# Attention and gated MLP on one core: the second product's matmuls taken block by block, exponentials planned into the buffer that is free first, and every step put in a new order

## The chip, the cores and the metric

The kernel runs on one core of a Trainium2 chip. A core has a matrix engine (TensorE, PE in the profile; its weight loads are PEld), VectorE (DVE), ScalarE (ACT), GpSimd (POOL) and SyncE (SP, which here issues all DMAs). Each engine works through its own instruction queue in order and waits on semaphores for the others. The metric is the device time of one execution in microseconds (us), the median of several runs.

## The reference, cut to what matters

```python
def _attn_ref(q, k, v, g_q, g_k):            # batch 8, heads 12, seq 448, head_dim 64
    q_n, k_n = rmsnorm(q, g_q), rmsnorm(k, g_k)
    scores = matmul(q_n, k_n.transpose(0, 1, 3, 2)) / sqrt(64)
    attn = exp(scores - max(scores))
    attn = attn / (sum(attn) + 1e-9)
    return matmul(attn, v)
...
def _moe_ref(x, w_in, conv_w, w_out):        # x 8 x 448 x 768, w_in 768 x 1024, w_out 1024 x 768
    h = maximum(x @ w_in, 0.0)
    conv_out = 3-tap convolution of h along the sequence, one set of taps per column
    gate = 1.0 / (1.0 + exp(-conv_out))
    return (h * gate) @ w_out
```

## The kernel before, in words

The work is cut into small steps, each a function: a call for one tile on one engine. A helper `at(t, fn, ...)` puts a step on a list with a due time made of a formula in `PH`, `PACE` and a shift per kind of step (`SHIFT`). A planner at the end of the kernel then builds one order for each engine: it keeps, for every engine, the steps whose predecessors (`needs`) are placed, adds up planned costs (`options`: a step's planned time on each engine that may take it; `LAT`: the planned delay from one engine to another; `OVER`: the part of a step's planned time by which the next step on the same engine may overlap it), and places the step that can start first, with due times weighted by `beta`. What it builds is an order and nothing else: on the chip each engine takes its instructions in that order and waits where an operand is late.

Heads go two at a time, a pair n (48 pairs, six to a batch). For a pair, q and k are loaded and normalised (`square`, `square_sum`, `rsqrt`, `apply_rms`), transposed by PE (`qk_transpose`) or, for q of later pairs, by a DMA (`q_turn`), and split into a high and a low float16 part (`qk_hi`, `qk_lo`). `scores(n, g)` multiplies them into PSUM for the row blocks of 128 queries, seven blocks j = 0..6 to a pair. Each block goes through `soft_max` (DVE, the row's negated maximum), `soft_exp` (ACT, into one of four buffers with tag `e`), and is then turned: in pairs 0 to 9 all blocks by PE (`p_transpose`, copied out of PSUM by `p_evac`), from pair 10 on the first six (even pairs) or five (odd pairs) by a split into two float16 halves (`p_hi`, `p_lo`) and a DMA (`p_turn`), and only the last block or two by PE. `pv(n, i)` multiplies with v, `x_scale` divides by the row sums (which come back through DRAM, tile rB), `x_hi` and `x_lo` split the result in two float16 parts, tile x.

The MLP of batch b: `in_part(b, fc, j, w)` is w matmuls of the first product for column block fc (0..7); its index i runs over the six pairs' x (i // 3) and for each over three terms: high times high, low times high, high times low (table `T3`). Six such steps fill one PSUM bank. Then `in_relu`, three steps `in_conv`, `in_tanh`, `in_gate`, which frees the bank, and `in_hi`, `in_lo`, which write the gated block in two parts g into a ring of slots (`gring` and two spare places). The second product, `out_part(b, ch, half, j, w)`, takes 24 matmuls in six steps of four for each output tile. Its order before, line 909, is term by term: all eight blocks of the high part, then the low parts, then the high parts with the low weights, so that its second step already needs block 7. All matmul outputs share eight PSUM banks, which are handed out by the planner: a step that takes a bank waits until the last reader of its former content is done.

Weights w_in and w_out are loaded, converted and bounded at the start (`load`, `convert`, `bound`, `bound_max`, `bound_turn`, `bound_spread`, `scale`, `split`, `rest`) between the attention steps of the first pairs.

Two lines that the change replaces and the prediction uses, with the planned costs of before:

```python
            soft_exp=lambda: [act(0.645)],
...
    OVER = dict(PE=0.0, DVE=0.08, ACT=0.1, POOL=0.035)
```

## Time and profile before

| | us |
|---|---|
| median of 3 runs | 844.54 |
| lowest and highest | 844.24 and 846.04 |
| span of the profiled execution | 844.4 |
| PE busy in it | 799.5 |
| DVE, ACT, POOL busy | 701.8, 698.1, 517.7 |

The profiled execution's span, from the first to the last instruction, is within 0.2 us of the median, so the trace's sums can be set against the median directly. A busy share is the part of the span in which at least one instruction of that engine was in flight; PE's matmuls overlap each other, so its busy time contains short waits that no gap shows. The start of one instruction to the start of the next (the pitch) is what a matmul really takes.

### The profile page before, as it was taken

The page shows a single profiled execution, that of the slowest core. Times are in us where ns is not written, and L with a number is a line of the kernel's source. Part 1 is how long each engine was busy: PE and PEld are TensorE (multiplying, and loading weights), DVE is VectorE, ACT ScalarE, POOL GpSimd, SP SyncE. Part 2 cuts the span into 40 slices and gives each one's busy share as a digit, 9 for nine tenths or more (in the row PEclk, how much of TensorE's full clock was granted, in tenths as well). Part 3 has the DMA queues.
Part 4 walks back from the last instruction along what each step waited for, and adds up shares of the span by engine and source line. Part 5 has one row for each costly group of instructions (what it writes and reads, how often), then busy time and mean ns, then how long its engine had stood idle before and what let it go on. Part 6 is the DMA issues. An engine that isn't in the chain of part 4 may idle for free.

```text
span 844.4 us, 17078 instructions
## 1 busy us (share of the span) xinstructions
PE 799.5 (95%) x5650; PEld 435.0 (52%) x5650; DVE 701.8 (83%) x1298; ACT 698.1 (83%) x1647; POOL 517.7 (61%) x633
## 2 busy tenths in 40 slices
PE   3897999999999999999999999999999999999998
PEld 2454455545554555555555555555545555555554
DVE  7889988997899889998889988998789989781430
ACT  4889999989899887999898987998898987893441
POOL 4445246487678667597577767697667767572120
PEclk9998999999999999999999999999999999999999
DMA  9684553169997899869997898979996899555001
GB/s 255 180 197 122 172 147 109 45 137 197 180 194 173 163 193 200 167 141 196 197 177 161 182 200 186 179 150 199 183 187 154 185 184 169 108 106 112 10 18 58
DMA packets 325640, 132.47 MB, mean 157 GB/s; under 512 B 265312, under 2 KB 321968, under 8 KB 325552
## 3 DMA queue, kind: packets, MB, share of 16 engines
q1 hardware_dynamic: 325552, 131.39, 75.0%
q8 instruction: 44, 0.72, 0.4%
q14 instruction: 44, 0.36, 0.1%
HBM read 56.65 MB, written 11.18 MB: 80 GB/s over the span
## 4 chain that ended last, share of the span: by engine, by line
PE 38%; ACT 24%; DVE 17%; DMA 9%; issue 7%; POOL 4%; SPq 2%; ACTq 0%; DVEq 0%; POOLq 0%
PE bank L917 15%; PE bank L848 8%; PE bank L764 6%; PE bank L642 5%; DMA rB<-rd 4%; ACT ph L98 3%; PE bank L686 3%; ACT sq L385 2%; DMA PT<-ph 2%; DMA wo<-in_moe_w_in_dram 2%; DVE vp L748 1%; ACT PT L98 1%; POOL ph L110 1%; ACT bank L856 1%; SPq L678 1%
## 5 line engine op out<-in xcount | busy, mean ns | idle before, releaser
L848 PE MATMUL bank<-x,wi 128*128 128x448 f16 x1152 | 233.8, 353 | 0.0
L917 PE MATMUL bank<-wo,gring 128*128 128x384 f16 (+1 forms) x1056 | 203.4, 327 | 1.8 <-DVE c_(0_7_1979 L878 1.7
L848 PEld LDWEIGHTS <-wi 128*128 128x128 f16 x1152 | 110.9, 98 | 99.3 <-issue 7.6
L917 PEld LDWEIGHTS <-gring 128*128 128x128 f16 (+1 forms) x1056 | 101.6, 99 | 67.6 <-issue 16.3
L642 PE MATMUL bank<-kT,qT 64*128 64x448 f16 (+3 forms) x1072 | 131.8, 395 | 4.1 <-ACT qT L98 3.4
L764 PE MATMUL bank<-PT,vp 112*64 112x448 f16 x912 | 93.7, 354 | 0.8 <-DVE c_(5_4_8472 L878 0.4
L110 POOL TENSOR_TENSOR x<-x,x 128x448 f16<-128x448 f32 x48 | 52.9, 1102 | 45.3 <-ACT x L98 33.3
L110 POOL TENSOR_TENSOR sq<-qkf,st 112x512 f32<-112x512 f32 x61 | 72.1, 1191 | 8.5 <-DVE st L417 5.1
L764 PEld LDWEIGHTS <-vp 112*64 112x64 f16 x912 | 50.2, 110 | 41.3 <-issue 12.6
L396 DVE TENSOR_REDUCE st<-sq 112x16 f32<-112x1024 f32 (+1 forms) x50 | 58.2, 1168 | 7.0 <-ACT sq L385 6.5
L642 PEld LDWEIGHTS <-qT 64*128 64x128 f16 (+1 forms) x912 | 32.7, 97 | 51.8 <-issue 32.1
L385 ACT ACTIVATE sq<-qkf 112x1024 f32<-112x1024 f32 (+1 forms) x50 | 51.1, 1022 | 4.2 <-DMA qkf<-in_q_dram 2.3
L917 PE MATMUL bank<-wo,wi 128*128 128x384 f16 (+1 forms) x192 | 46.9, 326 | 0.0
L456 PE MATMUL bank<-ident,sq 112*128 112x112 f32 x232 | 32.4, 267 | 14.4 <-POOL sq L110 13.9
L775 DVE TENSOR_TENSOR x<-bank,rB 128x448 f32<-128x448 f32 x38 | 23.6, 622 | 25.2 <-PE bank L764 9.9
L702 DVE TENSOR_TENSOR PT<-bank,PT 112x512 f16<-112x512 f32 x57 | 39.0, 684 | 4.3 <-ACT PT L98 3.9
L856 ACT ACTIVATE bank<-bank 128x448 f32<-128x448 f32 x64 | 34.1, 534 | 7.3 <-PE bank L848 6.6
L748 DVE SCALAR_TENSOR_TENSOR vp<-v,vsc,vp 112x512 f16<-112x512 f32 x38 | 39.8, 1047 | 0.2 <-ACT vp L102 0.2
L98 ACT COPY PT<-bank 112x512 f32<-112x512 f32 x64 | 36.9, 590 | 3.5 <-PE bank L686 3.4
L110 DVE TENSOR_TENSOR sq<-qkf,st 112x512 f32<-112x512 f32 x35 | 38.7, 1131 | 0.0
L709 POOL TENSOR_SCALAR rsum<-rsum 128x7 f32<-128x7 f32 x48 | 17.5, 365 | 33.5 <-ACT e_(3_6_774 L656 7.5
L98 ACT CAST x<-x 128x448 f16<-128x448 f32 x45 | 25.2, 560 | 15.5 <-DVE x L775 14.8
(2228 smaller groups left out, 2021.8 us busy)
## 6 DMA issues: line engine op xcount, KB each, us to landing
qkf<-in_k_dram SPq DMA_DIRECT2D x48, 224.0 KB
v<-in_v_dram SPq DMA_DIRECT2D x48, 224.0 KB
rB<-rd SPq DMA_DIRECT2D x96, 112.0 KB
wo<-in_moe_w_in_dram SPq DMA_DIRECT2D x12, 512.0 KB
gring<-in_moe_w_out_dram SPq DMA_DIRECT2D x16, 384.0 KB
qkf<-in_q_dram SPq DMA_DIRECT2D x24, 224.0 KB
qkf<-in_q_dram SPq DMA_DIRECT2D x48, 112.0 KB
PT<-ph SPq DMA_TRANSPOSE x209
```

Of the source, the lines that this page charges most:

```text
L98: (nc.scalar.copy if e == "ACT" else elementwise(e).tensor_copy)(dst, src)
L110: elementwise(e).tensor_tensor(dst, a, b, op=op)
L385: nc.scalar.activation(sq, x, AF.Square)
L396: nc.vector.tensor_reduce(st, sq, axis=AX.X, op=ALU.add)
L456: nc.tensor.transpose(ps[:, t * PB : (t + 1) * PB], x[:, t], ident[:PB, :PB])
L642: nc.tensor.matmul(ps[u][o, :S], lhs, rhs, start=(i == 0), stop=(whole(m) or i == 2),)
L702: nc.vector.tensor_tensor(turned(n, j, 1), held["t", ("p", n, j)][:PB].rearrange("p (k q) -> p k q", k=NB), turned(n, j, 0), op=ALU.subtract,)
L748: nc.vector.scalar_tensor_tensor(vp[:, 1], old("v", n), old("vsc", n // NP)[:PB, 1:2], vp[:, 0], op0=ALU.mult, op1=ALU.subtract,)
L764: nc.tensor.matmul(ps[HALF[h], :S], lhs, rhs, start=(i == 0 and k == 0), stop=(i == pvs(n)[-1] and k == NB - 1),)
L848: nc.tensor.matmul(ps[:, :S], wi[:, wl, c, fc * P : (fc + 1) * P], old("x", b * NP + c)[:, xl], start=(i == 0), stop=(i == 3 * NP - 1),)
L856: nc.scalar.activation(ps, ps, AF.Relu, scale=2.0 ** -24)
L917: nc.tensor.matmul(ps[p0 : p0 + m, :NO2], g, wo[:, wl, fc, half * NO2 : (half + 1) * NO2], start=(i == 0), stop=(i == 3 * NFC - 1),)
```

## The change

Three things change in the code and all numbers of the tables.

1. `out_part` walks a new list `OUT`: for each block fc its three terms (high with both weight parts, then low), where before it went term by term over all blocks. A step of four then needs the blocks up to (j + 3) // 3 only, and a slot of g is free for the next batch once the last two `out_part` steps that read its block are done; before, it was once the whole second product of the batch was done.
2. `needs` of `in_part` asks for the x of the pair that its matmuls read; before, it asked for the x of all six pairs. `x_hi` asks for the last `in_part` step that reads its own pair.
3. The planner's rule for the four exponential buffers changes: before, an exponential waited in the plan for the buffer of the exponential four places earlier; now it waits for the first one of those in use that is freed.
4. Planned costs (`options`, `LAT`), a factor for each engine (`COST`) and `PH`, `PACE`, `SHIFT` are all new, so all steps are placed anew.

```diff
-    sw=0.0, f_pl=0.052, f_ql=0.872, f_lo=0.172, f_rms=0.091, f_sq=0.309, T=17.368, ti=41.151,
+    sw=-0.0213, f_pl=0.0039, f_ql=-14.6094, f_lo=0.2593, f_rms=0.1033, f_sq=0.3016, T=17.5428,
...
+COST = dict(
+    PE=0.9855, DVE=1.0004, ACT=1.0007, POOL=1.0014,
+)
...
+    OUT = [(fc, gl, wl) for fc in range(NFC) for gl, wl in ((0, 0), (0, 1), (1, 0))]
...
-            gl, wl = T3[i // NFC]
-            fc = i % NFC
+            fc, gl, wl = OUT[i]
...
-            m, j = back(n, a[1], BUFS["e"])
-            yield ("p_lo" if j < nd(m) else "p_transpose"), m, j
...
-            yield "in_part", (n - BUFS["x"]) // NP, NFC - 1, 3 * NP - 3, 3
+            yield "in_part", (n - BUFS["x"]) // NP, NFC - 1, n % NP * 3, 3
...
-            for i in range(NP):
-                yield "x_lo", b * NP + i
+            for c in range(j // 3, (j + m - 1) // 3 + 1):
+                yield "x_lo", b * NP + c
...
-            pb = back(b, a[1], NGS, NFC)[0]
-            yield "out_part", pb, 3 if pb % 2 else 2, 1, 3 * NFC - 4, 4
-            yield "in_carry", *back(b, a[1], NGS, NFC)
+            pb, pf = back(b, a[1], NGS, NFC)
+            for half in range(2):
+                yield "out_part", pb, 3 if pb % 2 else 2, half, (3 * pf + 2) // 4 * 4, 4
+            yield "in_carry", pb, pf
...
-            soft_exp=lambda: [act(0.645)],
+            soft_exp=lambda: [act(0.725)],
...
-            p_low=lambda: [dve(0.63)],
+            p_low=lambda: [dve(0.683)],
...
-            in_part=lambda: [pe(0.58)],
+            in_part=lambda: [pe(0.568)],
...
-            out_part=lambda: [pe(0.67)],
+            out_part=lambda: [pe(0.65)],
...
-        "PE": dict(PE=0.0, DVE=0.2, ACT=0.2, POOL=0.2, SP=0.2, DMA=0.2),
+        "PE": dict(PE=0.0, DVE=0.2062, ACT=0.1869, POOL=0.8133, DMA=0.32, SP=0.32),
...
+                if step[0] == "soft_exp" and exps >= BUFS["e"]:
+                    if exps - BUFS["e"] >= len(freed):
+                        continue
+                    t = max(t, back_at(freed[exps - BUFS["e"]], e, dma))
...
+        c = c if dma else c * COST[e]
```

The same 4976 steps are placed, 1265 of them on PE with the same matmuls. Which engine takes an elementwise step changes for a few dozen: among others `out_evac` moves from DVE to ACT five times and `sum_evac` eleven times, twelve `in_carry` go from ACT to DVE, five `q_lo` from DVE to POOL, three `apply_rms` from POOL to DVE. PE changes between kinds of products (`scores`, `pv`, everything else) 271 times before and 289 times now.

What moves is seen at three places of PE's queue. Line numbers of after are 4 or 5 higher than those of before for the same statement. The first place is the transposition of the last block of pair 38, e_(38_6. L642 (L646) are `scores`, L848 (L853) `in_part`, L686 (L690) `p_transpose`. Before:

```order
L642 MATMUL bank_67<-kT_7973,qT_8029 64x448
...
L642 MATMUL bank_73<-kT_7973,qT_8029 128x448
...
L848 MATMUL bank_69<-x_7933,wi_84 128x448
...
L848 MATMUL bank_68<-x_7011,wi_84 128x448
...
L686 MATMUL bank_66<-ident,e_(38_6_8224 112x128 x4
...
L848 MATMUL bank_68<-x_7316,wi_84 128x448
```

And after, at the same place:

```order
L853 MATMUL bank_70<-x_7945,wi_84 128x448
...
L853 MATMUL bank_66<-x_7033,wi_84 128x448
...
L460 MATMUL bank_73<-ident,sq_7891 128x112 x4
...
L853 MATMUL bank_66<-x_7288,wi_84 128x448
...
L646 MATMUL bank_71<-kT_8003,qT_8058 128x448
...
L853 MATMUL bank_66<-x_7506,wi_84 128x448
...
L853 MATMUL bank_66<-x_7726,wi_84 128x448
...
L853 MATMUL bank_73<-x_6826,wi_84 128x448
...
L690 MATMUL bank_68<-ident,e_(38_6_8255 112x128 x4
```

Before, the block's own scores (the rows with 64 in them hold half of it), one more scores step and two `in_part` steps of three matmuls stand ahead of the transposition; now the block's scores lie ahead of everything shown, and twelve `in_part` steps (not all shown), a `qk_transpose` and a scores step stand between.

The second place is the start of batch 0's second product, L917 (L921), on the banks that it is written to. Before:

```order
L642 MATMUL bank_72<-kT_1864,qT_1737 128x448
...
L917 MATMUL bank_67<-wo_85,gring 128x384
...
L456 MATMUL bank_66<-ident,sq_1606 128x112 x4
L686 MATMUL bank_70<-ident,e_(10_6_2032 112x128 x4
...
L917 MATMUL bank_73<-wo_85,gring 128x384
...
L917 MATMUL bank_67<-wo_85,gring 128x384
```

After:

```order
L768 MATMUL bank_72<-PT_1611,v_735 64x448 x8
...
L921 MATMUL bank_69<-wo_85,gring 128x384
...
L690 MATMUL bank_68<-ident,e_(10_6_2021 112x128 x4
L460 MATMUL bank_71<-ident,sq_1768 128x112 x4
...
L646 MATMUL bank_72<-kT_1758,qT_1655 128x448
...
L921 MATMUL bank_69<-wo_85,gring 128x384
L921 LDWEIGHTS gring
L921 MATMUL bank_71<-wo_85,gring 128x384
```

Before, one step of the first output tile is followed by a step into bank_73, the bank that held the first product's block 7; now four steps of the first tile come first, the second tile goes to bank_71, and no block of the first product is the last user of either bank.

The third place is the first `in_part` of the kernel, about 95 to 125 us into the span, among the transpositions of pairs 5 to 7. Before:

```order
L686 MATMUL bank_70<-ident,e_(5_4_1047 112x128 x4
L642 MATMUL bank_73<-kT_973,qT_1002 128x448
...
L686 MATMUL bank_70<-ident,e_(5_5_1061 112x128 x4
L686 MATMUL bank_69<-ident,e_(5_6_1071 112x128 x4
L686 MATMUL bank_68<-ident,e_(6_0_1092 112x128 x4
...
L686 MATMUL bank_73<-ident,e_(7_4_1279 112x128 x4
L848 LDWEIGHTS wi_84
L848 MATMUL bank_71<-x_618,wi_84 128x448
```

After:

```order
L690 MATMUL bank_72<-ident,e_(5_4_1047 112x128 x4
...
L853 MATMUL bank_68<-x_533,wi_84 128x448
...
L853 MATMUL bank_68<-x_738,wi_84 128x448
L690 MATMUL bank_66<-ident,e_(5_5_1063 112x128 x4
L719 MATMUL bank_71<-ident,rsum_940 7x128
...
L853 MATMUL bank_68<-x_847,wi_84 128x448
...
L690 MATMUL bank_70<-ident,e_(5_6_1073 112x128 x4
```

Before, the first `in_part` follows block 4 of pair 7; now three steps of it stand between blocks 4 and 6 of pair 5, and three more between there and block 4 of pair 7.

## Rows read from the trace of the kernel before

**Rows 1.** The page's first part: engine, busy us (share), instructions.

```profile
PE 799.5 (95%) x5650; PEld 435.0 (52%) x5650; DVE 701.8 (83%) x1298; ACT 698.1 (83%) x1647; POOL 517.7 (61%) x633
```

**Rows 2.** Busy time by stage: stretch, length, then each engine; PEclk is the granted clock.

```profile
0.00:10.32 10.32, 0.00 (x0) 0.00 (x0) 6.08 (x24) 4.10 (x7) 3.87 (x14) 1.00 0.73 210
10.32:130.00 119.68, 104.12 (x595) 58.15 (x596) 110.75 (x238) 107.63 (x270) 53.15 (x80) 0.96 0.68 177
130.00:800.00 670.00, 654.44 (x4771) 353.04 (x4768) 576.87 (x1026) 572.88 (x1348) 455.46 (x535) 1.00 0.81 160
800.00:844.40 44.40, 40.90 (x289) 23.80 (x287) 8.10 (x13) 13.50 (x25) 5.18 (x5) 1.00 0.10 36
```

**Rows 3.** Timeline of PE, 742 to 757 us: start, us, instruction, count.

```profile
742.82 3.00 PE L848 MATMUL bank<-x,wi 128*128 128x448 f16 x15
745.66 0.27 PE L715 MATMUL bank<-ident,rsum 128*7 128x128 f32 x1
745.86 1.43 PE L642 MATMUL bank<-kT,qT 64*128 64x448 f16 x18
...
752.86 3.42 PE L917 MATMUL bank<-wo,gring 128*128 128x384 f16 x20
756.12 0.27 PE L715 MATMUL bank<-ident,rsum 128*7 128x128 f32 x1
756.23 2.76 PE L917 MATMUL bank<-wo,gring 128*128 128x384 f16 x16
```

**Rows 4.** PE's waits from 130 to 800 us: us in total, times, longest.

```profile
PE bank L917 <- DVE c_(0_7_1979 L878: 1.7, 1, 1.7
...
PE bank L686 <- ACT e_(13_5_2619 L656: 1.0, 1, 1.0
PE bank L686 <- ACT e_(38_6_8224 L656: 0.9, 1, 0.9
...
PE bank L917 <- ACT e_(16_5_3316 L656: 0.4, 1, 0.4
...
PE bank L686 <- ACT e_(29_5_6234 L656: 0.2, 1, 0.2
```

**Rows 5.** Timeline of ACT, 626 to 627 us: one exponential and what follows it.

```profile
626.20 0.66 ACT L656 ACTIVATE e_(39_3_8368<-bank,sst_(39_3_8352 128x448 f32<-128x448 f32 x1
...
626.82 0.58 ACT L98 CAST gring<-c_(5_1_8288 128x448 f16<-128x448 f32 x1
```

**Rows 6.** Timeline of PE, 180 to 187 us, where batch 0's second product starts.

```profile
180.58 0.65 PE L686 MATMUL bank<-ident,e_(10_6_2032 128*112 128x128 f32 x4 [0.18 <-ACT e_(10_6_2032 L656]
182.93 4.06 PE L917 MATMUL bank<-wo,gring 128*128 128x384 f16 x24 [1.70 <-DVE c_(0_7_1979 L878]
```

**Rows 7.** Timelines of DVE and PE, 65 to 78 us, and one stretch's busy row.

```profile
65.10 0.61 DVE L648 TENSOR_REDUCE sst_(3_5_725<-bank 128x1 f32<-128x448 f32 x1
...
68.13 0.27 PE L190 MATMUL bank<-ident,wred_in 128*1 128x128 f32 x1 [3.46 <-DVE wred_in L287]
...
72.22 1.10 PE L686 MATMUL bank<-ident,e_(3_3_671 128*112 128x128 f32 x4
...
77.74 0.65 PE L686 MATMUL bank<-ident,e_(4_0_818 128*112 128x128 f32 x4
78.23 0.60 PE L686 MATMUL bank<-ident,e_(4_1_824 128*112 128x128 f32 x4
...
72.22:75.82 3.60, 3.60 (x18) 3.26 (x17) 3.40 (x11) 2.80 (x6) 2.02 (x5) 0.50 1.09 227
```

**Rows 8.** Timeline of PE, 120 to 126 us; last, the w_in halves on line L312.

```profile
120.53 1.02 PE L642 MATMUL bank<-kT,qT 64*128 64x448 f32 x4 [1.07 <-ACT qT L98]
...
123.74 1.86 PE L848 MATMUL bank<-x,wi 128*128 128x448 f16 x9
...
L312 DVE SCALAR_TENSOR_TENSOR wi<-wi,wsc x6: 1270/1284/1511, 75.0 to 96.7; 128x1024 f16<-128x1024 f32 x6
```

**Rows 9.** All waits, one of DVE's rows.

```profile
DVE x L775 <- DMA rB<-rd: 9.4, 10, 2.6
```

More of the change, by code (lines that the diff above doesn't have):

```diff
@@ L28 @@
+    p_qh=1.3778, p_ql=5.1453, p_ph=15.3737, p_pl=18.0701,
 )
 PACE = [
-    19.684, 19.21, 17.229, 18.732, 12.899, 14.504, 12.3, 10.264, 22.811, 17.751, 23.834, 17.246,
+    19.6835, 17.2279, 17.1001, 19.4583, 13.0839, 14.5901, 12.3383, 10.1304, 23.241, 17.8279, 22.0846, 15.8073,
 ]
 SHIFT = dict(
-    prepare=49.118, load_g=66.183, make_g=161.271, load_cw=41.777, make_cw=228.436, load=30.589,
-    convert=88.08, bound=185.211, bound_max=505.945, bound_turn=109.494, bound_row=36.478,
-    bound_spread=103.145, scale=368.594, in_factor=602.484, split=143.452, rest=-5.433,
@@ L36 @@
-    out_factor=26.564, load_k=207.53, load_q=-22.481, square=411.214, square_sum=340.919,
-    rsqrt=50.152, apply_rms=498.265, qk_transpose=555.031, qk_hi=86.942, v_load=355.244,
-    v_bound=-7.228, scores=24.319, soft_max=-4.096, soft_exp=21.811, p_transpose=365.136,
-    p_evac=1.005, sum_add=366.28, sum_step=2.99, sum_transpose=104.607, sum_evac=262.686,
-    sum_store=184.116, sum_load=7.026, pv=384.832, x_scale=90.761, x_hi=276.516, x_lo=5.432,
-    v_max=-27.973, v_turn=484.625, v_row=103.578, v_spread=219.686, v_scale=143.146,
@@ L42 @@
-    qk_lo=-5.353, q_hi=-16.467, q_lo=93.092, q_turn=368.336, p_hi=513.085, p_lo=-4.651,
-    p_turn=292.059, p_low=-2.554, v_hi=204.989, v_lo=184.473, moe_scales=122.854,
-    in_part=120.167, in_relu=338.096, in_conv=209.998, in_tanh=27.902, in_gate=21.022,
-    in_hi=197.514, in_lo=1.938, in_carry=175.792, out_scales=185.546, out_part=267.736,
-    out_evac=257.905, out_store=1.003,
+    prepare=695.9036, load_g=605.045, make_g=537.5802, load_cw=507.761, make_cw=1158.5217,
+    load=31.6554, convert=120.3172, bound=646.657, bound_max=1897.893, bound_turn=288.6078,
@@ new lines @@
+    bound_row=964.8649, bound_spread=187.7733, scale=1072.724, in_factor=1018.0854,
+    split=742.8313, rest=-5.4893, out_factor=1386.2035, load_k=292.4823, load_q=-22.4572,
+    square=669.9932, square_sum=728.8853, rsqrt=1200.7674, apply_rms=1327.5481,
+    qk_transpose=1487.4879, qk_hi=51.7292, v_load=195.6348, v_bound=-6.2815, scores=102.7029,
+    soft_max=-4.2547, soft_exp=175.5778, p_transpose=64.7604, p_evac=0.5117, sum_add=63.9685,
+    sum_step=1281.1798, sum_transpose=442.8909, sum_evac=286.0047, sum_store=534.9805,
@@ new lines @@
+    sum_load=-0.73, pv=279.316, x_scale=196.1933, x_hi=1476.0933, x_lo=5.043, v_max=-27.0337,
+    v_turn=1369.8103, v_row=682.245, v_spread=716.8841, v_scale=1686.192, qk_lo=-11.3264,
+    q_hi=-16.4621, q_lo=1098.9752, q_turn=1358.9663, p_hi=431.7814, p_lo=-5.142, p_turn=7.7804,
+    p_low=-1.725, v_hi=856.9811, v_lo=140.521, moe_scales=314.8581, in_part=1449.2977,
+    in_relu=1462.579, in_conv=787.5631, in_tanh=144.9106, in_gate=772.8823, in_hi=507.0311,
+    in_lo=4.5699, in_carry=174.6416, out_scales=357.2239, out_part=29.3667, out_evac=289.1293,
@@ L47 @@
+    out_store=-6.4416,
+)
+COST = dict(
+    PE=0.9855, DVE=1.0004, ACT=1.0007, POOL=1.0014,
 )
@@ L1250, in needs @@
             yield "in_lo", *a
-            yield "out_part", b - 3, 0, 1, 3 * NFC - 4, 4
+            for half in range(2):
+                yield "out_part", b - 3, 0, half, 3 * NFC - 4, 4
         elif name == "out_part":
@@ L1309, in options @@
             v_scale=lambda: [dve(0.7)],
-            scores=lambda: [pe(0.77 if whole(a[0]) else 0.585)],
+            scores=lambda: [pe((0.912 if whole(a[0]) else 0.691) if a[0] % 2 and not a[1] else 0.847 if whole(a[0]) else 0.578)],
             soft_max=lambda: [dve(0.62)],
-            soft_exp=lambda: [act(0.645)],
-            p_transpose=lambda: [pe(0.455)],
-            p_low=lambda: [dve(0.63)],
-            p_evac=lambda: [act(0.59), dve(0.62)],
+            soft_exp=lambda: [act(0.725)],
+            p_transpose=lambda: [pe(0.436)],
+            p_low=lambda: [dve(0.683)],
+            p_evac=lambda: [act(0.585), dve(0.682)],
             sum_add=lambda: [pool(0.3), dve(0.09)],
@@ L1431, in tile_attention_moe, with frees_e @@
     ringq = {"m": [], "c": [], "t": [], "s": []}
+    exps, freed = 0, []
+    def frees_e(name, *a):
+        return name == "p_transpose" and a[1] >= nd(a[0]) or name == "p_lo"
     most = dict(s=PH["cs"], t=PH["ct"], m=PH["cm"], c=BUFS["c"])
@@ L1518, in tile_attention_moe @@
                     last_in[i] = g
+        exps += step[0] == "soft_exp"
+        if frees_e(*step):
+            freed.append(step)
         order.append(step)
```

63 lines of the change are left out of this document (31 added, 32 removed).

## The prediction

> **What bounds the kernel now.** I read the page's busy shares first. PE is in flight for 799.5 of 844.4 us; DVE, ACT and POOL lie 140 us and more below it [rows 1]; weight loads, 52%, run beside the matmuls. By stage [rows 2] that splits in four. Until 10.32 us PE has nothing. From 10.32 to 130 us PE idles 15.6 us (119.68 less 104.12) while DVE and ACT are busy for 93% and 90% of the stretch: there those two set the pace. From 130 to 800 us PE idles 15.6 us more, and DVE and ACT have 14% free. The last 44.4 us are PE alone, with 3.5 us of evacuation and store behind it. So a new order can give back some of about 31 us of visible idle time, plus what hides inside PE's busy time.
>
> For that the pitch is needed [rows 3]. Fifteen matmuls of the first product take 745.66 - 742.82 = 2.84 us, 189 ns each, 0.568 us a step of three. Twenty of the second take 756.12 - 752.86 = 3.26 us, 163 ns each, 0.652 us a step of four. One such matmul is in flight for 0.33 to 0.35 us, so each of PE's waits hides another 0.17 us or so in the busy time. The same rows price a change between kinds of products: the transposition of the row sums takes 0.11 us when a full product follows (756.12 to 756.23) and 0.20 us when scores follow (745.66 to 745.86), so 0.09 us for the change.
>
> **Where PE waits from 130 to 800 us.** The list of PE's waits [rows 4] has 26 entries that add up to 15 us. Sixteen of them, from 1.0 to 0.2 us and 9.6 us together, are `p_transpose` (L686) waiting for the exponential of block 5 or 6. The four matmuls of such a step are in flight for 0.65 us where the next step can start 0.49 us after them [rows 7], so each wait hides another 0.16 us: about 12 us in all. Three waits of L917 and two of L642, 0.2 to 0.4 us, are for the bank of a late exponential; two of L764 are of 0.4 us, not shown; and the largest, 1.7 us, is batch 0's second product waiting for `in_gate` of block 7.
>
> Why the exponentials are late can be worked out. Before, the plan gave one 0.645 us less the overlap of 0.1, so 0.545 us of ACT; the trace gives 626.82 - 626.20 = 0.62 us [rows 5]. Seven to a pair make 0.5 us that ACT falls behind its plan. PE was planned too slow: 0.67 against 0.652 and 0.58 against 0.568 us [rows 3], with eight steps of each to a pair (384 over 48 pairs) 0.14 + 0.10 = 0.24 us. PE comes 0.76 us early to a transposition for each pair's work, and the larger waits, 0.7 to 1.2 us with their hidden part, have that size. The new costs are 0.725 less 0.1, 0.65 and 0.568 us, the trace's own.
>
> **The change part by part.** The matmuls are the same, so the pitch costs nothing.
>
> *Changes of kind*: 289 instead of 271, 18 at 0.09 us: +1.7 us. Nothing hides this, PE being the bound.
>
> *Transpositions placed by true costs*: of about 12 us, between none (the waits only move to the next step) and all can go. In PE's queue, counted with the pitches above, the work between a block's scores and its transposition grows from 1.9 to 8.1 us for e_(38_6 and from 1.9 to 6.1 us for e_(13_5, of the rows shown; of the nine largest waits six get at least 0.7 us more, two stay within 0.2 us, one (18_6) drops from 5.0 to 2.1 us. I take six in ten: -7 us, the rest staying because DVE's and ACT's durations vary more than a plan can know.
>
> *Second product block by block*: the start of batch 0's [rows 6] costs 182.93 - 180.58 = 2.35 us where a transposition's four matmuls take 0.49, so 1.9 us. Now four steps of the first output tile (2.6 us) come first, no bank of it is one that the first product's last block held, and the step that needs block 7 has 12.9 us of PE's work between it and that block, where it had 7.6. The same holds for the waits of L917 in odd batches, of 0.2 to 0.4 us, with 0.17 us hidden in each. Bounds 0 and 3.2 us; -2.5 us, nearest to the one row with a whole mechanism. That a slot of g frees earlier is worth nothing: no row of PE's waits is for a slot.
>
> *Early part*: `bound_turn` waits 3.46 us for DVE's maximum [rows 7]. In DVE's new queue three instructions less stand ahead of it, two maxima of 0.61 us and a conversion: -1.5 us, bounds 0 and -3.46. [...]
>
> *First product earlier*: it starts at 123.74 us, although w_in's last part, 1.3 us long, began at 96.7 us [rows 8], because its rule wanted the x of all six pairs. Six steps of 0.568 us now stand ahead of that place, in a stretch where PE waits on ACT, at 120.53 us for 1.07 us. 3.4 us of work can lie in idle time that lasts anyway; I take -2 us. If w_in is not ready, those steps wait and hold the transpositions behind them: loss to 1 us.
>
> *Other waits* (L642, L764) go by the same cause: -1 us of 1.4.
>
> *New waits*: an `in_part` that takes the bank of a `pv` stands at least 1.3 us of PE's work behind it, and eight do so where four did, at 3.0 us or more; that bank is free once `x_scale` is done, and `x_scale` itself waits for rB, 9.4 us in ten times and 2.6 us at worst [rows 9]. The last pair's x has 14 us of PE's work before its use in the middle case, where it had 21. Between 0 and 2.6 us at each; I allow +2 us in all, since before, DVE's waits for rB delayed no PE step in the list.
>
> *Buffers of exponentials*: no instruction changes, and ACT has 14% free; 0 us. Moves of `out_evac`, `sum_evac` and others between DVE and ACT are under 12 of 1280 steps and change neither share: 0 us while both have that room, and some 5 us at 0.3 to 0.6 us each if they had not.
>
> *Sum*: 844.4 + 1.7 - 7 - 2.5 - 1.5 - 2 - 1 + 2 = 834.1 us. The profiled execution stands within 0.2 us of the median, so I predict **834 us**, its own range 828 to 840.
>
> **The rivals.**
>
> *Nearly all waits go.* The 12 us of transpositions, 3.2 of the second product, 3.46 and 1.6 us at `bound_turn`, 3.4 us of filled idle time and 1.4 us of others: 844.4 + 1.7 - 25.1 = 821.0 us. For it speaks that the error of the plan has just the size of the waits; against it that 18_6 moves closer and that DVE and ACT stay the pace until 130 us.
>
> *Slower: PE stops for x.* The queue is strict, so an `in_part` that waits for a bank of `pv` or for the last pair's x holds every transposition behind it, and ACT and DVE run dry after. Sixteen places (eight banks, eight batches) at 1.5 us each are 24 us in place of the 2 allowed: 844.4 + 1.7 - 14 + 24 = 856 us. It decides from 0.8 us a place on, where sixteen waits make up the 14 us of gains less the 1.7. The spacing of 1.3 us and the waits for rB speak for it; against it, that most of the sixteen have 5 us and more.
>
> *No change.* ACT and DVE, not the plan's error, make the exponentials late: then each wait comes back at the next transposition and only the second product's gain, the changes of kind and half of the new waits remain: 844.4 + 1.7 - 2.5 + 1 = 844.6, within 0.2% of before, which is about what a measurement of this kernel can tell from no change. Their 14% of free time speaks against it.
>
> **How the numbers follow.** The forecast (828 to 840) has 0.60; nearly all waits gone, or between it and the forecast, 0.15; a gain that stays smaller (840 to 842.8) 0.07; no change 0.05; slower 0.13. Faster by over 0.2% is then 0.60 + 0.15 + 0.07 = 0.82, same 0.05, slower 0.13. The range leaves out the lowest tenth, below 821, and the worst tenth, above 848.
>
> **What would show it.** In the changed profile PE's idle time from 130 to 800 us is 5 to 9 us instead of 15.6; the L686 waits for e add up to 4 us instead of 9.6; no wait of 1.7 us stands at the start of a second product; `bound_turn` waits near 2 us; the first `in_part` starts before 105 us; DVE's, ACT's and POOL's busy sums stay within 1%. Wrong it would be made by waits of L848 for x or for `x_scale`, by L686 waits that keep their sum under other names, or by a longer early stretch.

## The result, and the profile after

The changed kernel takes **834.03 us** (median; 831.97 to 835.67), where 834 was predicted. The kernel before ran beside it at 844.39 us; the ratio is 0.9882, 95% interval 0.9854 to 0.9909. A second comparison, later, gave 834.92 against 843.18 us, 0.9908 (0.9884 to 0.9932). The change makes the kernel about 1% faster.

The page's first part, as in [rows 1]:

```profile
PE 800.4 (96%) x5650; PEld 433.6 (52%) x5650; DVE 701.7 (84%) x1293; ACT 697.2 (84%) x1646; POOL 512.5 (61%) x639
```

The work is the same; no engine's sum moved by more than about 1%. More steps change their engine than the net numbers told, 205 of the 4976 (`rsqrt` goes from DVE to POOL 40 times and back 35 times), but they cancel in these sums. Busy time by stretch of the changed kernel, as in [rows 2], and behind it three short stretches that are used below:

```profile
10.32:130.00 119.68, 111.39 (x632) 60.64 (x632) 115.42 (x250) 111.70 (x281) 52.62 (x90) 0.97 0.68 183
130.00:800.00 670.00, 659.60 (x4809) 355.41 (x4809) 579.11 (x1020) 575.15 (x1347) 454.12 (x535) 1.00 0.80 159
800.00:833.90 33.90, 29.45 (x216) 17.58 (x210) 1.54 (x3) 6.35 (x11) 2.07 (x2) 0.97 0.13 47
...
0.00:61.00 61.00, 46.03 (x263) 24.63 (x263) 55.03 (x138) 49.46 (x124) 25.74 (x50) 1.00 0.84 232
...
64.00:70.00 6.00, 5.80 (x22) 4.16 (x23) 5.90 (x13) 5.08 (x13) 0.75 (x3) 0.50 0.81 172
...
242.00:250.00 8.00, 5.59 (x26) 2.35 (x24) 7.93 (x12) 5.28 (x15) 4.27 (x5) 0.79 0.53 103
```

PE idles 8.3 us before 130 us (119.68 less 111.39; it was 15.6) and 10.4 us from 130 to 800 us (15.6). By 130 us it has done 632 matmuls instead of 595. PE's waits from 130 to 800 us, against [rows 4]:

```profile
PE bank L646 <- DVE PT L706: 2.2, 1, 2.2
PE bank L460 <- POOL sq L114: 1.9, 2, 1.6
PE bank L690 <- ACT e_(44_6_9598 L660: 1.0, 1, 1.0
PE bank L690 <- ACT e_(12_6_2425 L660: 0.8, 1, 0.8
PE bank L690 <- ACT e_(20_6_4221 L660: 0.7, 1, 0.7
...
PE bank L853 <- ACT e_(14_5_2840 L660: 0.4, 1, 0.4
PE bank L690 <- ACT e_(30_6_6496 L660: 0.4, 1, 0.4
PE bank L690 <- ACT e_(43_6_9410 L660: 0.3, 1, 0.3
PE bank L690 <- ACT e_(25_6_5345 L660: 0.2, 1, 0.2
```

Transpositions (L690) wait in six places for 3.4 us, where it was sixteen for 9.6. No wait for `in_gate` and none of the second product is left in the list. The largest wait, 2.2 us for a low half of PT, has no counterpart before. The second, 1.6 us for a normalised q/k, has one in the list of the kernel before, which the prediction's account of that list leaves out:

```profile
PE bank L456 <- POOL sq L110: 1.2, 1, 1.2
```

The timeline of PE at the places of [rows 6 to 8]:

```profile
61.00 0.27 PE L194 MATMUL bank<-ident,wred_in 128*1 128x128 f32 x1 [0.47 <-DVE wred_in L291]
62.62 1.02 PE L646 MATMUL bank<-kT,qT 64*128 64x448 f32 x4 [1.36 <-ACT qT L102]
...
94.26 1.31 PE L853 MATMUL bank<-x,wi 128*128 128x448 f16 x6
...
170.07 3.23 PE L768 MATMUL bank<-PT,v 112*64 112x448 f32 x16
173.23 2.77 PE L921 MATMUL bank<-wo,gring 128*128 128x384 f16 x16
```

`bound_turn` comes at 61.00 us (68.13) and waits 0.47 us (3.46); the first product starts at 94.26 us (123.74); the second starts at 173.23 us right behind the product with V, with no wait.

**A finer count.** Idle rows miss what a wait hides inside busy time, so I used pitches, for all kernels alike: the distance from each PE step's first matmul to the next step's, less that step's undisturbed distance in the trace (0.567 us `in_part`, 0.650 `out_part`, 0.436 `p_transpose`, 0.757 the product with V; 750.2 us for all steps) and less 0.093 us where the kind changes. What is left is put down to the step that came late, and to the stretch in which the wait for it began. Spans then split exactly: PE's start 10.3 to 10.6, changes of kind 25.2 to 26.9, lost before 130 us 28.1 to 21.3, lost from 130 to 800 us 26.4 to 20.0, lost behind that, the last output's way out included, 4.1 to 5.0; together 844.4 to 833.9. One order run again gives another few us: the order of before, in another kernel below, lost 25.9, 23.2 and 4.1 us. Single differences under 3 us are not read.

### The profile page after: what moved, and what is told of

It reads as the page before. It is cut to its first block, busy times and chain, and to the rows that moved or that the text cites. A ratio compares the mean times of both kernels' runs of the same rounds, so it can differ in the third digit from the quotient of the medians.

```text
span 833.9 us, 17046 instructions
## 1 busy us (share of the span) xinstructions
PE 800.4 (96%) x5650; PEld 433.6 (52%) x5650; DVE 701.7 (84%) x1293; ACT 697.2 (84%) x1646; POOL 512.5 (61%) x639
## 5 line engine op out<-in xcount | busy, mean ns | idle before, releaser
L853 PE MATMUL bank<-x,wi 128*128 128x448 f16 x1152 | 234.8, 354 | 0.5 <-ACT e_(14_5_2840 L660 0.4
L921 PE MATMUL bank<-wo,gring 128*128 128x384 f16 (+1 forms) x1056 | 187.8, 326 | 0.0
L853 PEld LDWEIGHTS <-wi 128*128 128x128 f16 x1152 | 110.0, 98 | 103.5 <-issue 14.9
L646 PE MATMUL bank<-kT,qT 64*128 64x448 f16 (+3 forms) x1072 | 134.3, 393 | 6.0 <-ACT qT L102 2.7
L921 PEld LDWEIGHTS <-gring 128*128 128x128 f16 (+1 forms) x1056 | 101.4, 99 | 61.7 <-issue 9.6
L114 POOL TENSOR_TENSOR x<-x,x 128x448 f16<-128x448 f32 x48 | 50.9, 1061 | 44.8 <-ACT x L102 39.3
L114 POOL TENSOR_TENSOR sq<-qkf,st 112x512 f32<-112x512 f32 x58 | 66.6, 1157 | 8.9 <-DVE st L421 2.2
L646 PEld LDWEIGHTS <-qT 64*128 64x128 f16 (+1 forms) x912 | 32.5, 97 | 52.2 <-issue 32.8
L114 POOL TENSOR_TENSOR qkf<-sq,qkf 112x512 f16<-112x512 f32 x34 | 43.2, 1271 | 9.9 <-ACT qkf L102 9.5
L460 PE MATMUL bank<-ident,sq 112*128 112x112 f32 x232 | 33.2, 268 | 15.7 <-POOL sq L114 14.8
L779 DVE TENSOR_TENSOR x<-bank,rB 128x448 f32<-128x448 f32 x38 | 23.6, 621 | 25.9 <-PE bank L768 19.4
L706 DVE TENSOR_TENSOR PT<-bank,PT 112x512 f16<-112x512 f32 x57 | 38.9, 683 | 7.1 <-ACT PT L102 6.8
L114 DVE TENSOR_TENSOR sq<-qkf,st 112x512 f32<-112x512 f32 x38 | 41.0, 1085 | 0.8 <-POOL st L424 0.5
L752 DVE SCALAR_TENSOR_TENSOR vp<-v,vsc,vp 112x512 f16<-112x512 f32 x38 | 40.8, 1076 | 0.5 <-ACT vp L106 0.4
L921 PE MATMUL bank<-wo,wi 128*128 128x384 f16 (+1 forms) x192 | 40.3, 327 | 0.0
L102 ACT COPY PT<-bank 112x512 f32<-112x512 f32 x68 | 39.1, 583 | 1.3 <-PE bank L690 1.0
L460 PEld LDWEIGHTS bank<-ident,sq 112*128 112x128 f32 x232 | 25.6, 143 | 26.6 <-POOL sq L114 16.4
```

The lines of the kernel that those rows point to most:

```text
L102: (nc.scalar.copy if e == "ACT" else elementwise(e).tensor_copy)(dst, src)
L114: elementwise(e).tensor_tensor(dst, a, b, op=op)
L460: nc.tensor.transpose(ps[:, t * PB : (t + 1) * PB], x[:, t], ident[:PB, :PB])
L646: nc.tensor.matmul(ps[u][o, :S], lhs, rhs, start=(i == 0), stop=(whole(m) or i == 2),)
L706: nc.vector.tensor_tensor(turned(n, j, 1), held["t", ("p", n, j)][:PB].rearrange("p (k q) -> p k q", k=NB), turned(n, j, 0), op=ALU.subtract,)
L752: nc.vector.scalar_tensor_tensor(vp[:, 1], old("v", n), old("vsc", n // NP)[:PB, 1:2], vp[:, 0], op0=ALU.mult, op1=ALU.subtract,)
```

## Experiments

**In the kernel before: one part alone.** Block by block, in the old order of steps:

```diff
-            gl, wl = T3[i // NFC]
-            fc = i % NFC
+            fc, gl, wl = i // 3, *((0, 0), (0, 1), (1, 0))[i % 3]
```

> The kernel before with its order of steps left as it was, and only the matmuls inside the second product taken block by block (all three terms of a block, then the next block). If block order by itself is what the term of 2.5 us was for, the start of the second product in batch 0 and the waits ahead of out_part shrink at once: 841 to 843 us, ratio near 0.997. If block order only allows a planner to begin earlier, and the gain lies in where the steps then stand, the position of every step is as before and the waits stay: 844 us, within 0.2% of before, with the waits ahead of out_part between 130 and 800 us still near 6 us.

842.87 against 842.91 us, ratio 0.9997 (0.9981 to 1.0013). Ahead of `out_part` it lost 5.4 us from 130 to 800 us (6.0 before), and the largest wait is the old one, 1.7 us for `in_gate` of block 7:

```profile
181.10 4.06 PE L916 MATMUL bank<-wo,gring 128*128 128x384 f16 x24 [1.69 <-DVE c_(0_7_1979 L878]
```

By itself the matmuls' order is worth nothing. The step that waits here, as in the kernel before, is the first of the second output tile, the one into bank_73. Block by block it reads only blocks 0 and 1, so it waits for the bank that `in_gate` frees and not for block 7's data: this wait was one of the banks' hand-out, not of the order of the matmuls.

**The suspected cause alone.** If transpositions merely stand too early, they can be put later by hand:

```diff
+    where = {s: k for k, s in enumerate(order)}
+    moved = {}
+    for s in order:
+        if s[0] == "p_transpose" and s[1] >= 10:
+            moved.setdefault(min((x for x in after[s]), key=where.get), []).append(s)
+    gone = {s for v in moved.values() for s in v}
+    order = [x for s in order if s not in gone for x in (*moved.get(s, ()), s)]
+    SCHED["order"] = order
```

> The kernel before with each transposition of exponentials of pairs 10 and up put 1 to 3 places of the program later, to just ahead of the first step that needs it; nothing is planned anew and no other step moves. The theory that transpositions stand too early for exponentials that take longer than the old plan gave them: the 13.9 us of waits ahead of transpositions between 130 and 800 us fall to 4 to 8, and the time to 835 to 840 us (ratio 0.990 to 0.995). The rival that ScalarE is simply behind and TensorE meets the same wait one step on (at the product with V or the next scores): transpositions wait less but other steps wait as much more, 843 to 846 us.

848.23 us, ratio 1.0063 (1.0040 to 1.0085): slower than either theory said. Ahead of transpositions 4.7 us are lost instead of 13.9, as the first theory has it; but ahead of `out_part` 11.5 instead of 6.0, of the product with V 3.8 instead of 1.2, of `v_spread` 2.2 instead of nothing, and changes of kind cost 1.4 us more. PE's waits from 130 to 800 us in this kernel show who is late next:

```profile
PE bank L917 <- DVE c_(0_7_1979 L878: 2.5, 1, 2.5
PE bank L198 <- DVE mx L193: 2.1, 1, 2.1
PE bank L917 <- ACT gring L98: 1.7, 2, 0.9
```

And the waits of ACT and DVE in the same stretch:

```profile
ACT PT L98 <- PE bank L686: 11.5, 21, 2.7
...
DVE PT L702 <- ACT PT L98: 10.5, 19, 2.0
```

In the kernel before these two are:

```profile
ACT PT L98 <- PE bank L686: 3.4, 8, 0.9
...
DVE PT L702 <- ACT PT L98: 3.9, 13, 0.9
```

A transposition that comes later makes ACT wait for its bank, and DVE for ACT's copy, since their queues kept their order; what stands behind in those queues (a step of the gate, a maximum, a copy into gring) comes late for PE. The rival was right in kind: moving one engine's steps alone moves the wait, and here it grew on the way.

**The durations without the search.** The kernel before with the changed kernel's durations and latencies and the old phases, paces and shifts:

```diff
-            soft_exp=lambda: [act(0.645)],
+            soft_exp=lambda: [act(0.725)],
...
-            in_part=lambda: [pe(0.58)],
+            in_part=lambda: [pe(0.568)],
...
-            out_part=lambda: [pe(0.67)],
+            out_part=lambda: [pe(0.65)],
...
+        c = c if dma else c * COST[e]
```

> The planner of the kernel before with its old search numbers (phases, paces, shifts), its own matmul order and rule for the exponentials' buffers, but with the changed kernel's durations and latencies: a plan anew with the trace's durations alone. If the durations carry the gain, 832 to 838 us (ratio 0.985 to 0.993), with waits ahead of transpositions under 8 us between 130 and 800 us. If what counts is the search over phases and shifts, which was done for each set of durations, this plan is no better or is worse: 845 to 870 us, with new waits in places where neither kernel has them.

852.14 us, ratio 1.0113 (1.0087 to 1.0139). Transpositions lose 8.4 us (13.9 before), but 34.0 us go before 130 us (28.1), some 4 of them in one wait at the end of that stretch, where the first `in_part` wants a bank that DVE frees late:

```profile
130.03 2.40 PE L851 MATMUL bank<-x,wi 128*128 128x448 f16 x6 [3.94 <-DVE PT L101]
```

Durations alone do not carry the gain.

**The changed kernel's new waits.** They lie close together: between the first scores of pair 13 and of pair 17 (199 to 269 us) it loses 9.1 us, where the kernel before loses 1.7 (203 to 267 us); in the rest of 130 to 800 us it loses 10.9, before 24.8. The timeline there, first DVE, then POOL, then PE:

```profile
239.96 4.05 DVE L752 SCALAR_TENSOR_TENSOR vp<-v,vsc,vp 112x512 f16<-112x512 f32 x1
243.94 0.68 DVE L706 TENSOR_TENSOR PT<-bank,PT 112x512 f16<-112x512 f32 x1
...
239.45 1.04 POOL L114 TENSOR_TENSOR ph<-e_(14_3_2774,ph 128x448 f16<-128x448 f32 x1
240.45 1.03 POOL L114 TENSOR_TENSOR ph<-e_(14_4_2795,ph 128x448 f16<-128x448 f32 x1
241.44 1.04 POOL L114 TENSOR_TENSOR ph<-e_(14_5_2840,ph 128x448 f16<-128x448 f32 x1
242.43 1.03 POOL L114 TENSOR_TENSOR ph<-e_(15_0_2913,ph 128x448 f16<-128x448 f32 x1
...
241.13 1.30 PE L853 MATMUL bank<-x,wi 128*128 128x448 f16 x6
244.67 0.36 PE L646 MATMUL bank<-kT,qT 64*128 64x448 f16 x1 [2.23 <-DVE PT L706]
245.20 1.27 PE L646 MATMUL bank<-kT,qT 64*128 64x448 f16 x5 [0.17 <-DVE x L779]
246.41 2.22 PE L853 MATMUL bank<-x,wi 128*128 128x448 f16 x6
```

The low half of v for pair 14 (L752), usually 0.75 us, takes 4.05 and ends 0.55 us behind the last of POOL's four tensor_tensors; the PT behind it frees the bank late, scores wait 2.23 us for that, and behind that idle time the granted clock falls: 0.79 on average from 242 to 250 us, 0.50 from 245.2 to 248.0, six matmuls in 2.22 us where six took 1.30. Put later by hand, with one more step of that kind near 201 us:

```diff
+    for s, behind in [(('v_lo', 14), ('x_scale', 13)), (('out_scales', 1), ('soft_max', 13, 1))]:
+        order.remove(s)
+        k = order.index(behind) + 1
...
+        order.insert(k, s)
+    SCHED["order"] = order
```

> The changed kernel with two steps of VectorE put later in its order (28 of 4976 places differ): the low half of v of pair 14 behind x_scale of pair 13, and the scales of the output of batch 1 behind the running maximum of pair 13, second step. In the changed kernel these two instructions took 4.05 us and 2.00 us while GpSimd ran tensor_tensors back to back, and TensorE then waited 2.2 and 0.8 us and lost some 2 us more to a lower granted clock. If these two instructions are the cause of the cluster of waits between 195 and 250 us, it shrinks from about 8 to 3 or 4 us: 829 to 831 us, ratio to before 0.982 to 0.984. If whatever VectorE does while GpSimd runs so is stretched, another instruction takes the delay and the time stays: 833 to 835 us, ratio 0.987 to 0.989.

833.33 against 842.91 us, ratio 0.9883 (0.9861 to 0.9906), no different from the changed kernel's. The timeline of DVE here:

```profile
240.95 0.69 DVE L706 TENSOR_TENSOR PT<-bank,PT 112x512 f16<-112x512 f32 x1 [0.45 <-ACT PT L102]
241.59 0.63 DVE L779 TENSOR_TENSOR x<-bank,rB 128x448 f32<-128x448 f32 x1
242.13 3.35 DVE L752 SCALAR_TENSOR_TENSOR vp<-v,vsc,vp 112x512 f16<-112x512 f32 x1
```

And the busy row of the stretch that had 5.59 us of PE and a clock of 0.79 in the changed kernel:

```profile
242.00:250.00 8.00, 7.87 (x47) 3.67 (x46) 7.96 (x11) 5.55 (x16) 4.52 (x5) 1.00 0.85 158
```

The instruction is stretched as before (3.35 us), but PT no longer stands behind it: PE is busy for 7.87 of the 8 us from 242 to 250 us, at a granted clock of 1.00. That wait is explained. Over pairs 13 to 16 the loss goes from 9.1 to 6.3 us only, since PE then waits 1.2 us for an exponential of pair 15 and the like, and in the time nothing is to be seen.

**The same plan with one number moved by a thousandth, old durations, term by term.** These ran on one chip with the changed kernel. Its own repetition:

> The changed kernel itself once more, beside the three plans below on one chip. Both theories: ratio to the kernel before 0.985 to 0.991, and in its second trace the same waits at the same places (the 4 us instruction of VectorE near 240 us, TensorE's waits of 2.2 us behind it), if they belong to the order of the steps; if those waits were an accident of one execution they are elsewhere.

834.92 us, 0.9908 (0.9884 to 0.9932), with the same largest wait. From the list of PE's waits and from DVE's timeline:

```profile
PE bank L646 <- DVE PT L706: 2.2, 1, 2.2
```

```profile
239.15 4.05 DVE L752 SCALAR_TENSOR_TENSOR vp<-v,vsc,vp 112x512 f16<-112x512 f32 x1
```

The waits belong to the order. Now the nudge:

```diff
-    PE=0.9855, DVE=1.0004, ACT=1.0007, POOL=1.0014,
+    PE=0.9855, DVE=1.0004, ACT=1.0017, POOL=1.0014,
```

> The changed kernel with one number of its planner moved by a thousandth (ScalarE's factor 1.0007 to 1.0017, so 0.6 ns on an exponential); nothing that the plan knows of durations is truly different, but the steps are planned anew and fall out another way. The theory that true durations carry the gain: the plan is as good, 832 to 837 us, ratio 0.986 to 0.992. The rival that the gain lies in one order out of many, picked by a search whose phases and shifts fit that one order: the plan loses 4 to 15 us, 838 to 850 us, with new waits of 1 to 4 us in places where the changed kernel has none.

846.13 us, ratio 1.0030 (1.0014 to 1.0046): all of the gain is gone. Transpositions (5.5 us), `out_part` (1.5) and the start (20.9) stay as in the changed kernel; other steps lose 21.0 us instead of 14.4. The largest new wait, on PE's timeline:

```profile
224.54 0.72 PE L646 MATMUL bank<-kT,qT 64*128 64x448 f16 x5 [0.54 <-ACT e_(14_2_2711 L660]
229.68 0.98 PE L460 MATMUL bank<-ident,sq 112*128 112x112 f32 x4 [4.41 <-ACT qkf L102]
```

q of pair 16 is normalised late. Then three old durations in the changed kernel:

```diff
-            soft_exp=lambda: [act(0.725)],
+            soft_exp=lambda: [act(0.645)],
...
-            in_part=lambda: [pe(0.568)],
+            in_part=lambda: [pe(0.58)],
...
-            out_part=lambda: [pe(0.65)],
+            out_part=lambda: [pe(0.67)],
```

> The changed kernel with three durations of its plan set back to the old values: the exponential 0.645 instead of 0.725 (less 0.1 each in the plan), a step of in_part 0.58 instead of 0.568, one of out_part 0.67 instead of 0.65. If these durations were what removed the waits ahead of transpositions, those waits return between 130 and 800 us (10 to 14 us instead of 4.8) and the time is 838 to 845 us, clearly above the plan that was only moved by a thousandth. If one order out of many carries the gain, it loses no more than that plan does, and its waits are not ahead of transpositions above all.

853.92 us, ratio 1.0128 (1.0103 to 1.0152), 7.8 us above the nudge. But the waits that my theory says should return did not: transpositions lose 7.8 us, not 10 to 14; the loss is in the product with V (9.5 us) and at the same normalisation (5.5 us). Nor is it no more than the nudge's, as the rival had it. And term by term, with a slot of g freed again only when the whole second product of its batch is done:

```diff
-    OUT = [(fc, gl, wl) for fc in range(NFC) for gl, wl in ((0, 0), (0, 1), (1, 0))]
+    OUT = [(fc, gl, wl) for gl, wl in T3 for fc in range(NFC)]
...
-                yield "out_part", pb, 3 if pb % 2 else 2, half, (3 * pf + 2) // 4 * 4, 4
+                yield "out_part", pb, 3 if pb % 2 else 2, half, 3 * NFC - 4, 4
```

> The changed kernel planned anew with the second product term by term again (a group needs all eight blocks of the gated rows at its start, as in the kernel before). If block by block is worth the 2.5 us of my sum, this plan loses 1 to 4 us more than the plan moved by a thousandth, and TensorE waits for the last blocks ahead of out_part at the starts of the second product (3 us or more between 130 and 800 us; 0.85 in the changed kernel). If it is worth nothing, its loss is that of any plan made anew, and the waits ahead of out_part stay under 2 us.

857.79 us, ratio 1.0170 (1.0148 to 1.0192), 11.7 us above the nudge. `out_part` loses 13.6 us, where every plan block by block with the new tables loses 0.7 to 3.1. What it waits for is mostly not the last blocks, as I expected (0.4 us for one), but banks of late exponentials. The run takes back the order and the earlier freeing of slots together and does not tell the two apart. PE's waits from 130 to 800 us, of it:

```profile
PE bank L768 <- ACT e_(16_5_3321 L660: 1.7, 1, 1.7
...
PE bank L921 <- ACT e_(16_4_3289 L660: 1.5, 1, 1.5
...
PE bank L921 <- ACT e_(34_4_7383 L660: 1.5, 1, 1.5
...
PE bank L921 <- DVE c_(3_7_5965 L883: 0.4, 1, 0.4
```

**Does the planner know which plan is good?** It adds up its own durations to an end of the whole plan. Another nudge, with an end near the changed kernel's, was to tell:

```diff
-    PE=0.9855, DVE=1.0004, ACT=1.0007, POOL=1.0014,
+    PE=0.9865, DVE=1.0004, ACT=1.0007, POOL=1.0014,
```

> The changed kernel with another number of its planner moved by a thousandth (TensorE's factor 0.9855 to 0.9865) and the steps planned anew: 3237 of 4976 places differ. The first such plan (ScalarE's factor) lost all of the gain. The planner itself says when its plan would end: 804.4 us for the changed kernel, 820.6 for the first plan moved by a thousandth, 806.1 for this one. If any plan made anew loses the gain, since the search numbers fit one order alone: 842 to 850 us. If the planner's own end, made with the trace's durations, tells which plan is good (the chip came 25 to 31 us later than it in the five plans run so far with these tables): 832 to 837 us, ratio 0.986 to 0.993.

844.38 us, ratio 1.0020 (1.0005 to 1.0035): the planner's end did not tell, and the gain is lost once more. It keeps the 2.2 us wait for PT near 240 us of the changed kernel and has others of its own: 2.1 us for the exponential e_(23_5 at 384 us, 1.6 us for a low half of v.

Next, `in_part` with all six x again:

```diff
-            yield "in_part", (n - BUFS["x"]) // NP, NFC - 1, n % NP * 3, 3
+            yield "in_part", (n - BUFS["x"]) // NP, NFC - 1, 3 * NP - 3, 3
...
-            for c in range(j // 3, (j + m - 1) // 3 + 1):
+            for c in range(NP):
```

> The changed kernel planned anew with the rule that a step of in_part needs all six blocks of x of its batch, not the blocks that it reads alone. The planner's own end is 808.1 us. By that: 834 to 839 us, with the first in_part near 120 us instead of 93 and 1 to 3 us more of waits before 130 us, if the earlier in_part is what the start of the changed kernel gains by; with no more waits before 130 us than in the changed kernel (21.3 us) if the early gain comes from the order around bound_turn and the scores. If any plan made anew loses the gain: 842 to 850 us.

839.98 us, ratio 0.9965 (0.9951 to 0.9979), between the two forecasts. The first `in_part` comes at 117.01 us. Before 130 us it loses 23.6 us, 2.3 more than the changed kernel and 2.3 less than the least of the kernel before's order (25.9); 1.4 of the 2.3 us are one wait for an exponential of pair 8 that ends at 131.75 us.

A plan searched anew, with two more of DVE's steps marked for the planner as ones that can't run beside POOL's (`square`, the third new name, never runs on DVE), and all phases, paces and shifts moved:

```diff
-        "convert", "rest", "q_hi", "q_lo", "rsqrt", "in_carry", "moe_scales",
+        "convert", "rest", "q_hi", "q_lo", "rsqrt", "in_carry", "moe_scales", "square", "out_scales", "sum_step",
...
-    in_relu=1462.579, in_conv=787.5631, in_tanh=144.9106, in_gate=772.8823, in_hi=507.0311,
+    in_tanh=130.327139, in_gate=727.625657, in_hi=502.729006, in_lo=3.920174, in_carry=174.472305,
...
```

> The changed kernel with two of VectorE's steps (the scales of the output and the closing of a sum) told to the planner as steps that can't run beside GpSimd's, and its phases, paces and shifts searched anew from the changed kernel's values until the planner's own end came down from 808.5 to 803.7 us; 4324 of 4976 places differ from the changed kernel's. If the planner's end tells which plan is good: 829 to 835 us, as fast as the changed kernel or up to 4 us faster. If the changed kernel's order was one lucky draw whose short time the planner can't foresee: 840 to 850 us.

837.73 us, ratio 0.9941 (0.9919 to 0.9962): faster than before, some 3 us behind the changed kernel, though the planner gave it the earlier end; it lies between the two forecasts. Its transpositions lose 10.8 us; the largest wait is 3.2 us for one exponential at 566 us. Last, a nudge of the kernel before:

```diff
-            p_transpose=lambda: [pe(0.455)],
+            p_transpose=lambda: [pe(0.4555)],
```

> The kernel before with one duration of its plan moved by a thousandth (a step of p_transpose 0.455 to 0.4555) and planned anew; 2711 of 4976 places differ. The planner's own end goes from 827.6 to 830.5 us. If the planner's end tells, also with the old durations: 845 to 848 us, ratio 1.002 to 1.006. If the kernel before was as finely drawn as the changed one looked beside its first neighbour: 850 to 860 us, ratio 1.008 to 1.02. If its durations are so far from the trace that the draw means little: 840 to 845 us, either side of before.

848.19 us, ratio 1.0057 (1.0036 to 1.0078), just above the planner's 3 us more: 15.7 us ahead of transpositions, as in its parent, and 3 us more among the rest.

All kernels side by side, by the finer count (us lost in the profiled execution; the planner's end where the steps were planned anew; times are medians, the kernel before took 844.4, 842.9, 843.2 and 843.0 us in the four sets, and the profiled executions of the two nudged plans of the changed kernel, TensorE's and ScalarE's, ran 1.3 and 2.9 us below their medians):

```
                        planner  time   before 130  transp.  out_part  others
                                                    (130 to 800 us)
before                   827.6   844.4     28.1      13.9      6.0      6.6
block by block alone             842.9     25.9      11.1      5.4      6.6
transpositions later             848.2     27.2       4.7     11.5     11.2
before, nudged           830.5   848.2     26.6      15.7      4.1      9.7
before, new durations    822.8   852.1     34.0       8.4      7.0     10.1
changed kernel           804.4   834.0     21.3       4.8      0.9     14.4
  again                          834.9     21.7       5.2      0.9     12.5
  two steps moved                833.3     21.9       5.9      0.9     11.3
  searched anew          803.7   837.7     21.0      10.8      3.1     11.1
  all six x              808.1   840.0     23.6       6.9      1.0     13.2
  nudged, TensorE        806.1   844.4     21.1       7.8      0.7     18.8
  nudged, ScalarE        820.6   846.1     20.9       5.5      1.5     21.0
  old durations          827.9   853.9     24.8       7.8      2.0     24.3
  term by term           827.3   857.8     21.5       5.6     13.6     21.0
```

Two things are to be seen. The first three columns of losses mostly hold from plan to plan with the new tables. The last does not: it is 13 to 24 us in the plans that differ from the changed kernel's by a thousandth of one number, by one rule or by three durations, from 6.6 before, and in the two nudged plans it is what loses the gain. The planner's end sorts the plans with the new tables roughly (804 from 827), not within 5 us or so: 803.7 to 808.1 came out at 834.0 to 844.4.

## Why the prediction was right, point by point

The time, 834 us, was met to 0.03 us, but by terms that were off on both sides and made up for each other, so that closeness is luck. What the prediction had right is that the old waits go and by roughly how much. By the finer count, in order of the sum (what was measured adds up to 833.9 - 844.4 = -10.5 us; each term is rounded by itself):

- *Changes of kind*, +1.7: measured 26.9 - 25.2 = +1.7.
- *Transpositions*, -7: -9.1 (13.9 to 4.8). Six listed waits are left of sixteen, 3.4 us against the 4 foretold. The size is near; the cause that I worked out, the plan's short exponential, is not shown. With the new durations in the old search the loss falls to 8.4, but with the old durations in the new search it is 7.8, inside the 4.8 to 10.8 of the other new plans. Nor does the work that stands between a block's scores and its transposition decide it: e_(18_6, for which it fell, no longer waits, and e_(20_6, for which it rose from 2.9 to 6.6 us, still waits 0.7 us. What removed these waits, durations, search or the new rule for the exponentials' buffers, stays open; the rule was taken back in no run.
- *Second product*, -2.5: -5.1 ahead of `out_part` (6.0 to 0.9). Mis-sized, above my upper bound of 3.2. Alone, block by block gave nothing; within a new plan, taking it back together with the earlier freeing of slots, which I had put at nothing, cost 12 us ahead of `out_part`. It is room for a plan, and I priced it by the one place with a wait for `in_gate`, which was a wait for a bank and did not go with the order of the matmuls.
- *Early part*, -1.5, and *first product earlier*, -2: together -6.9 (28.1 to 21.3), of which `bound_turn`'s wait is -3.0 (3.65 to 0.63). I counted three instructions less ahead of the maximum on DVE; DVE's busy time ahead of it did fall by 3.0 us (58.0 in 68.13 us to 55.0 in 61.00), and its idle time by 4.2 more. The fall of the granted clock behind it stayed: 0.50 from 70.00 to 75.82 us before, 0.50 from 64 to 70 us now, after PE had waited 0.47 and 1.36 us. The steps at the low clock lost some 3.5 us before and 3.2 us now. The 1.6 us at `bound_turn` in the sum of "nearly all waits go" were my estimate for this low clock from four transpositions alone (3.60 us less four times 0.49, [rows 7]); no run shows them gained: the wait shrank, the low clock came all the same, and the loss at it hardly changed. Of the early `in_part`, taking back its rule cost 2.3 us before 130 us in the one plan that tried, near my 2, but within the scatter, and 1.4 of it is the wait for an exponential named above.
- *Other waits* -1 and *new waits* +2: measured +7.8 for all other steps from 130 to 800 us (6.6 to 14.4). This is the step that failed, and in its place too: I looked for the new waits at `in_part` behind a bank of the product with V or the last pair's x, and L853 waits once, 0.4 us, for the bank of an exponential. They came where the new order sets a normalisation of q and k, a low half of v and a POOL run against each other. Of these the list behind [rows 4] showed one, the 1.2 us for a normalised q/k, and I passed over it. So PE idles 10.4 us from 130 to 800 us, where I had said 5 to 9.
- PE's later start (+0.3) and a later end of the tail (+0.8) were not in the sum.

Of the signs that I named, the first product before 105 us, no wait at the start of the second product, the L690 sum and the busy sums within 1% (POOL's fell by just that) came true; `bound_turn`'s wait was below the 2 us foretold.

Of the rivals, "nearly all waits go" came nearest to what the old waits did: outside pairs 13 to 16 the loss from 130 to 800 us fell from 24.8 to 10.9 us. "PE stops for x" was in the wrong place, yet its kind, new waits that eat the gain, is what every plan made anew shows, by 3 to 18 us over the 6.6 of before. The chance of 0.13 that I gave to slower was too small for a plan taken at random: of six plans made anew from the changed kernel with something altered, four were slower than before, though two of these four also had old durations or the old order of the second product. That the changed kernel's own plan was one of the good ones could not be read from the trace of before.

No version here beats the changed kernel; with two steps moved it is level with it.

## What to carry to other kernels

When an order is planned anew, price the old waits from the trace and the new ones from the scatter of plans: move one irrelevant number by a thousandth, run it, and take that spread as the uncertainty of any gain that a re-ordering shows. A change that gives a planner room can be worth nothing alone and something inside a plan, as block by block here, so it can't be priced by one wait that it seems to remove: look first whether that wait is for data or for a buffer. Moving the waiting engine's steps later without the order of the engines behind it only handed the wait on here.

## What the runs showed of the hardware

A short DVE instruction took longer where POOL ran one tensor_tensor behind the other: at 239.96 us 4.05 us instead of 0.75, over the rest of one and three more. Three of DVE's lines in the changed kernel, min, median and longest in ns:

```profile
L752 DVE SCALAR_TENSOR_TENSOR vp<-v,vsc,vp x38: 696/750/4051, 187.0 to 745.2; 112x512 f16<-112x512 f32 x38
...
L706 DVE TENSOR_TENSOR PT<-bank,PT x57: 640/681/693, 180.6 to 754.7; 112x512 f16<-112x512 f32 x57
...
L779 DVE TENSOR_TENSOR x<-bank,rB x38: 608/624/643, 197.2 to 769.2; 128x448 f32<-128x448 f32 x38
```

L752, which reads no PSUM bank, is stretched up to 5.4 times (4051 against 750 ns); L706 and L779, of like size, which read one, never are (693 and 643 ns at the longest), though 32 and 24 of them ran beside a POOL tensor_tensor for over 0.4 us. Whether it is the bank that sets them apart no run tested. How far L752 is stretched beside a run of POOL instructions differs from place to place. At 239.96 us it ended 0.55 us behind the run (239.45 to 243.46 us); at 639.68 us it ended after 2.52 us while the run went on, and POOL's instruction there took 1.49 us instead of some 1.03. The timelines of DVE and POOL:

```profile
639.68 2.52 DVE L752 SCALAR_TENSOR_TENSOR vp<-v,vsc,vp 112x512 f16<-112x512 f32 x1
...
640.62 1.03 POOL L114 TENSOR_TENSOR ph<-e_(40_3_8640,ph 128x448 f16<-128x448 f32 x1
641.61 1.49 POOL L114 TENSOR_TENSOR ph<-e_(40_4_8658,ph 128x448 f16<-128x448 f32 x1
```

What decides between the two no run here shows. And a stall of 2.2 us on PE cost a further 2.0 us in the three steps behind it by the finer count (1.07, 0.53 and 0.39), at a granted clock of 0.79 from 242 to 250 us; without the stall the clock there was 1.00.
